# Twelve fp32r matmuls of four shapes in place of eight of the twelve bf16 warming matmuls, in an FNet mixing and feed-forward kernel

## The chip, the cores and the metric

One core of a Trainium2 chip. The time is the device time of one execution in microseconds, as a median over runs; the profile is of one execution, and its times count from the start of its span.

## What is computed

The input x is 2048 x 512, fp32. Two layers, each with a layer norm ahead and a residual around it:

```python
a = jnp.einsum("bsd,ed->bse", x, dft_hid_re)
b = jnp.einsum("bsd,ed->bse", x, dft_hid_im)
y = jnp.einsum("ts,bse->bte", dft_seq_re, a) - jnp.einsum("ts,bse->bte", dft_seq_im, b)
...
h = x + A(layernorm(x))                # A is the mixing above
h2 = h + (silu(layernorm(h) @ w1) @ w2)
```

The DFT matrices are inputs like any others: 2048 x 2048 for the sequence, 512 x 512 for the hidden dimension, each real and imaginary. w1 is 512 x 1792, w2 1792 x 512.

## The kernel before

The kernel keeps fp32 accuracy by splitting every operand into a rounded part and a remainder, both in fp32r, and forms each product by three matmuls: high weights with high moving data, high with low, low with high (`three`, lines 316 to 318). ScalarE makes the high part (line 266), VectorE the remainder (line 270, or 409 for the pieces of x). Every one of these matmuls has a weight tile of 128 x 128 and 512 moving columns. Block products are combined in the manner of Strassen: seven products in place of eight, with sums of blocks made on VectorE or by accumulating DMAs.

The stages follow each other on TensorE without a pause in the program: the mixing along the sequence (`plain(0, 0)`, then `fast` three times), the hidden mixing (`mix_fast`), and the up and down projections (`up`, `down`). A first part of `plain` takes the data as it arrives: the first tile of x and the first half-chunks of the sequence matrix are loaded (lines 468, 474 and 343), x is normalised (statistics at line 356, normalised high part at line 489, remainder at line 409), and TensorE does 4 + 4 + 4 products in three groups: high with high (line 513), high with the matrix's remainder (515), the remainder of x with high (517). Then it goes on with lines 316 to 318. `plain` then loads further pieces of x (line 343, `load_x`) and of the sequence matrix (line 442, `load_seq`), two of each per product.

The order of the work is written as events with times. `step` adds a stage of matmuls with work that leads it or follows it by so many microseconds; `at` adds a single piece of work. `MOVED` shifts each event by a number of its own, and the sorted list of events is the program's order, one and the same for all engines. Times in this list only sort; they make nobody wait.

Memory is 51 places of 4 KB per partition (`PAGES`). Every large tile is a "page". The program is run once against a stub, `Plan`, which notes for each page after how many uses it was requested and when it is used last by the list's times. `places` then gives each page, in the order of the requests, the free place that fell free earliest; fresh places come first:

```python
for taken, last in zip(self.taken, self.last):
    n = min((n for n in range(PAGES) if free[n][0] <= taken), key=lambda n: free[n][1])
    free[n] = last
```

A page in a used place waits at run time for the last reader of the page that was there before. A load that waits so holds up the SP queue, which issues nearly all loads, in order.

At the end of `program`, ahead of all events, come a few small pieces: three memsets on VectorE (`warm`, a bf16 tile of zeros, and two constants), one on GpSimd, and `WARM` = 12 matmuls of `warm` with itself into the first half of a PSUM tile `idle` that nobody reads (line 1357). They are the first work on TensorE.

Of the kernel before, what the change touches and what calls it, by code (L numbers as in the profile page):

```python
# [7 lines left out]
F32 = mybir.dt.float32  # L8
BF16 = mybir.dt.bfloat16
F32R = mybir.dt.float32r  # L10
# [5 lines left out]
P = 128  # L16
# [10 lines left out]
JJ = (2, 3, 0, 1)  # L27
EPS = 1e-5
PAGES = 51
WARM = 12  # L30
MM_US = 0.2265
PREP_US = 8.0
LEADS = (((0, 16, 8, 5.5), (1, 14, 5, 3.5), 12.5, 9),
# [149 lines left out]
class Plan:  # L183
# [5 lines left out]
    def page(self, name, dt=F32, shape=(2, 512)):  # L189
        self.taken.append(self.uses)  # L190
        self.last.append((self.uses, self.now))
        return Stub(self, len(self.taken) - 1)
# [14 lines left out]
def fnet_ffn_kernel(  # L207
# [18 lines left out]
    for plan.now, *_, f in program(stub, plan.page, stub, stub, stub, stub, x, xT, seq, hid, ffn, out):  # L226
        f()
    places = plan.places()

    def page(name, dt=F32, shape=(2, 512)):  # L230
        return pages.tile([P, *shape], dt, tag=f"pg{next(places)}", name=name)

    events = program(nc, page, keep, small, psum, dram, x, xT, seq, hid, ffn, out)


# [12 lines left out]
def program(nc, page, keep, small, psum, dram, x, xT, seq, hid, ffn, out):  # L248
# [11 lines left out]
    def banks(name):  # L260
        return psum.tile([P, 2, 512], F32, tag="ps", name=name)
# [1083 lines left out]
    up(1, 31, lambda: next(second[1]))  # L1345
    list(second[1])

    nc.vector.memset(warm, 0.0)
    nc.vector.memset(lower, -0.5 * EPS)
    nc.vector.memset(upper, EPS)  # L1350
    spare = keep.tile([P, 2], F32, name="spare")
# [3 lines left out]
    idle = banks("idle")  # L1355
    for _ in range(WARM):
        nc.tensor.matmul(idle[:, 0, :], warm[:, :P], warm, start=True, stop=True)

    return sorted(((t + MOVED.get(n, 0.0), at, n, f) for t, at, n, f in events), key=lambda v: v[:3])

# [33 lines left out]
```

## Time and profile before

| | us |
|---|---|
| median of 3 runs | 666.47 |
| lowest and highest run | 665.96, 666.97 |
| span of the profiled execution, first to last instruction | 664.2 |
| TensorE (PE) busy in that span | 657.6 |
| VectorE (DVE) busy | 575.7 |
| ScalarE (ACT) busy | 371.6 |
| GpSimd (POOL) busy | 97.8 |

The profile has one execution's instructions with start and length. "Busy" counts the time in which an engine executes, not that in which its sequencer waits or issues. PE is the matmuls, PEld the weight loads, which overlap them. A matmul's length in the profile is longer than its share of the engine, because the next one begins while it drains; the distance between two starts is what one costs. The span lies inside the device time; the profiled execution's own time outside the profiler isn't known, so the span of 664.2 us stands beside the median of 666.47 us, 2.3 us apart.

### The profile page before, as it was taken

What the parts mean: (1) busy time and instruction counts of PE and PEld (TensorE: products, weight loads), DVE (VectorE), ACT (ScalarE), POOL (GpSimd) and SP (SyncE); (2) the same over time, 40 slices, a digit from 0 to 9 for tenths busy, and PEclk for the clock granted to TensorE, in tenths of its full rate; (3) what the DMA queues carried; (4) which work ended last, traced back from release to release, by engine and by line L of the source; (5) the groups of instructions that cost most, each with busy time, mean ns of one, the idle gap of its engine ahead of it and who ended that gap; (6) DMA issues with size and microseconds to landing.
All of it is one profiled execution on the core that took longest, in us unless ns stands there. A gap on an engine that the chain in (4) does not pass through costs nothing.

```text
span 664.2 us, 8287 instructions
## 1 busy us (share of the span) xinstructions
PE 657.6 (99%) x2892; PEld 541.8 (82%) x2892; DVE 575.7 (87%) x727; ACT 371.6 (56%) x476; POOL 97.8 (15%) x128
## 2 busy tenths in 40 slices
PE   8999999999999999999999999999999999999997
PEld 5888888888888888888888888888888888888885
DVE  7999989898988999989999998988998854379964
ACT  6997456655445435364674555778543555664600
POOL 0011011111003434111121005343010000000000
PEclk9999999999999999999999999999999999999999
DMA  8981899999799586999999987669979645278803
GB/s 319 376 224 47 269 357 384 303 291 300 271 365 368 160 295 136 385 321 402 318 331 416 408 317 269 239 224 322 331 282 367 233 141 198 80 256 319 311 32 128
DMA packets 59706, 184.22 MB, mean 277 GB/s; under 512 B 6800, under 2 KB 13840, under 8 KB 59664
## 3 DMA queue, kind: packets, MB, share of 16 engines
q1 hardware_dynamic: 45456, 132.79, 54.8%
q0 software_dynamic: 13920, 50.63, 24.1%
q8 instruction: 23, 0.38, 0.3%
q10 hardware_dynamic: 288, 0.26, 0.1%
q14 instruction: 19, 0.16, 0.1%
HBM read 139.34 MB, written 44.32 MB: 277 GB/s over the span
## 4 chain that ended last, share of the span: by engine, by line
PE 98%; DMA 0%; DVE 0%; ACT 0%; issue 0%; DVEq 0%
PE m L317 11%; PE m L316 11%; PE m L318 11%; PE y L316 8%; PE y L318 8%; PE y L317 8%; PE f L318 6%; PE f L316 6%; PE f L317 6%; PE c L317 4%; PE c L318 4%; PE c L316 4%; PE vx L316 3%; PE vx L318 3%; PE vx L317 3%; PE c L517 1%
## 5 line engine op out<-in xcount | busy, mean ns | idle before, releaser
L266 ACT ACTIVATE ph<-raw 128x1024 fp32r<-128x1024 f32 x102 | 106.0, 1056 | 87.5 <-PE m L318 23.4
L270 DVE TENSOR_TENSOR pl<-raw,ph 128x1024 fp32r<-128x1024 f32 x88 | 112.1, 1289 | 9.1 <-ACT ph L266 7.1
L316 PE MATMUL m<-ph,S 128*128 128x512 f32 x192 | 74.7, 389 | 0.0
L317 PE MATMUL m<-pl,S 128*128 128x512 f32 x192 | 74.7, 389 | 0.0
L318 PE MATMUL m<-ph,S 128*128 128x512 f32 x192 | 74.7, 389 | 0.0
L316 PE MATMUL f<-gth,wf 128*128 128x512 f32 x161 | 62.6, 389 | 0.0
L317 PE MATMUL f<-gtl,wf 128*128 128x512 f32 x161 | 62.6, 389 | 0.0
L318 PE MATMUL f<-gth,wf 128*128 128x512 f32 x161 | 62.6, 389 | 0.0
L266 ACT ACTIVATE gth<-g 128x1024 fp32r<-128x1024 f32 x42 | 42.7, 1053 | 32.6 <-DVE g L1208 31.6
L270 DVE TENSOR_TENSOR gtl<-g,gth 128x1024 fp32r<-128x1024 f32 x42 | 50.3, 1219 | 7.0 <-ACT gth L266 5.7
L316 PE MATMUL m<-ph,X 128*128 128x512 f32 x144 | 56.0, 389 | 0.0
L317 PE MATMUL m<-pl,X 128*128 128x512 f32 x144 | 56.0, 389 | 0.0
L318 PE MATMUL m<-ph,X 128*128 128x512 f32 x144 | 56.0, 389 | 0.0
L1079 DVE TENSOR_TENSOR g<-vx,g 128x512 f32<-128x512 f32 x28 | 19.3, 689 | 30.5 <-PE vx L318 17.9
L714 DVE TENSOR_TENSOR raw<-raw,raw 128x1024 f32<-128x1024 f32 x36 | 43.9, 1221 | 0.5
L316 PE MATMUL y<-ph,hf 128*128 128x512 f32 x112 | 43.6, 389 | 0.0
L317 PE MATMUL y<-pl,hf 128*128 128x512 f32 x112 | 43.6, 389 | 0.0
L318 PE MATMUL y<-ph,hf 128*128 128x512 f32 x112 | 43.6, 389 | 0.0
L316 PEld LDWEIGHTS m<-ph,S 128*128 128x128 f32 x192 | 36.0, 188 | 7.5
L318 PEld LDWEIGHTS m<-ph,S 128*128 128x128 f32 x192 | 36.0, 188 | 7.5
L317 PEld LDWEIGHTS m<-pl,S 128*128 128x128 f32 x192 | 36.0, 188 | 7.4
L317 PEld LDWEIGHTS f<-gtl,wf 128*128 128x128 f32 x161 | 30.2, 188 | 6.3
(407 smaller groups left out, 1540.0 us busy)
## 6 DMA issues: line engine op xcount, KB each, us to landing
raw<-in_seq SPq DMA_DIRECT2D x84, 512.0 KB, 6.8
hf<-fd SPq DMA_DIRECT2D x28, 512.0 KB, 7.3
wf<-wd SPq DMA_DIRECT2D x28, 512.0 KB, 5.8
wf<-wd SPq DMA_DIRECT2D x28, 384.0 KB, 5.4
sf<-sd SPq DMA_DIRECT2D x18, 512.0 KB, 6.0
raw<-in_seq POOLq DMA_DIRECT2D x16, 512.0 KB, 6.9
fd<-hf POOLq DMA_DIRECT2D x14, 512.0 KB, 7.8
w<-in_ffn SPq DMA_DIRECT2D x23, 256.0 KB, 5.2
```

The costliest lines, as they stand in the source:

```text
L266: nc.scalar.activation(hi, src, AF.Copy, scale=sign)
L270: nc.vector.tensor_tensor(lo, src, hi, op=ALU.subtract)
L316: nc.tensor.matmul(acc, wh, mh, start=first, stop=False, skip_group_check=on)
L317: nc.tensor.matmul(acc, wh, ml, start=False, stop=False, skip_group_check=on)
L318: nc.tensor.matmul(acc, wl, mh, start=False, stop=last, skip_group_check=on)
L517: nc.tensor.matmul(o, wl, mh, start=False, stop=last)
L714: nc.vector.tensor_tensor(o, a, b, op=ALU.subtract)
L1079: nc.vector.tensor_tensor(g[q, f][:, tau, :], src, g[q, f][:, tau, :], op=ALU.add)
```

## The change

The twelve bf16 warming matmuls become four, unchanged in shape (128 x 128 weights, 512 columns). Behind them stand twelve new ones in fp32r, three of each of four shapes, written as (rows of weights, columns of weights, moving columns): (128, 128, 256), (128, 64, 512), (64, 128, 512), (128, 128, 512). They write the second half of the same PSUM tile, and nobody reads it. Their operand is the first half of a new page, `full`, which VectorE fills with zeros between the memset of `warm` and the two constants. The page comes from the same 51 places and is requested ahead of all others. The events and their order don't change.

```diff
-WARM = 12
+WARM = 4
+FORMS = (P, P, 256), (P, 64, 512), (64, P, 512), (P, P, 512)
...
+    full = page("full", F32)[:, 0, :]
     nc.vector.memset(warm, 0.0)
+    nc.vector.memset(full, 0.0)
+    full = full.bitcast(F32R)
     nc.vector.memset(lower, -0.5 * EPS)
     nc.vector.memset(upper, EPS)
...
     idle = banks("idle")
     for _ in range(WARM):
         nc.tensor.matmul(idle[:, 0, :], warm[:, :P], warm, start=True, stop=True)
+    for k, m, n in FORMS:
+        for _ in range(3):
+            nc.tensor.matmul(idle[:m, 1, :n], full[:k, :m], full[:k, :n], start=True, stop=True)
```

## The prediction

> **What bounds the kernel.** I read the page first: the span, the busy shares, the chain that ended last.
>
> ```profile
> span 664.2 us, 8287 instructions
> ...
> PE 657.6 (99%) x2892; PEld 541.8 (82%) x2892; DVE 575.7 (87%) x727; ACT 371.6 (56%) x476; POOL 97.8 (15%) x128
> ...
> PE 98%; DMA 0%; DVE 0%; ACT 0%; issue 0%; DVEq 0%
> ```
>
> TensorE is the bound, and 98% of the chain is matmuls. The next question is whether TensorE ever waits; the view of waits, for PE alone, answers it for the whole run:
>
> ```profile
> PE idle L1357 <- DVE upper L1350: 1.2, 1, 1.2
> PE c L513 <- DVE X L489: 0.5, 1, 0.5
> ```
>
> Two idle stretches: 1.2 us before the first warming matmul, 0.5 us between the warming and the first real one. So the case lies in the first ten microseconds, which the timeline shows (start, length, engine, line, operation, and in brackets the idle time before it and who ended it):
>
> ```profile
> 0.85 0.27 DVE L1348 MEMSET warm<- 128x256 uint32 x1 [0.85 <-PEq L1387]
> 1.18 4.23 PE L1357 MATMUL idle<-warm 128*128 128x512 bf16 x12 [1.18 <-DVE upper L1350]
> 1.58 0.15 PEld L1357 LDWEIGHTS <-warm 128*128 128x128 bf16 x1 [0.28 <-issue]
> 2.86 0.15 PEld L1357 LDWEIGHTS <-warm 128*128 128x128 bf16 x1 [0.28 <-issue]
> 3.26 0.75 DVE L356 BATCH_NORM_STATS2 st<-x 128x6 f32<-128x256 f32 x2 [2.12 <-DMA x<-in_x]
> 4.14 0.77 PEld L1357 LDWEIGHTS <-warm 128*128 128x128 bf16 x4 [0.28 <-issue]
> 5.35 0.73 DVE L489 TENSOR_SCALAR X<-x,mv,rs 128x256 fp32r<-128x256 f32 x2
> 5.91 1.17 PE L513 MATMUL c<-ph,X 128*128 128x512 f32 x4 [0.50 <-DVE X L489]
> 6.91 1.11 PE L515 MATMUL c<-pl,X 128*128 128x512 f32 x4
> 8.01 0.77 PEld L517 LDWEIGHTS c<-ph,X 128*128 128x128 f32 x4 [0.43 <-DVE X L409]
> 8.01 1.20 PE L517 MATMUL c<-ph,X 128*128 128x512 f32 x4
> 9.05 0.40 PE L316 MATMUL c<-ph,X 128*128 128x512 f32 x1
> ...
> 658.93 0.39 PE L318 MATMUL f4b<-gth,wf 128*128 128x512 f32 x1
> ```
>
> The weight loads start with their matmuls, so their starts give the pitch. While cold it is (4.14 - 1.58)/6 = 0.427 us; the four loads from 4.14 on lie in 0.77 us together, at most 0.77/3 = 0.26 us apart, about the half. So the rate doubled close to 4.15 us, 2.97 us after the first matmul. The column of the granted clock doesn't show this, so I trust the pitch:
>
> ```profile
> 2.00:4.00 2.00, 2.00 (x6) 0.76 (x5) 0.74 (x2) 0.64 (x2) 0.00 (x0) 1.00 0.78 266
> ```
>
> Of the 2880 real matmuls twelve start before 9.05 and the last at 658.93: 649.88/2867 = 0.2267 us each without a stall, to the end. Hence the rule of this case: **what moves the matmul at 9.05 moves the end by as much, and nothing before it counts.** From 5.91 to 9.05 are 3.14 us for 12 matmuls that need 12 x 0.2267 = 2.72; 0.42 us is slack. A first real matmul as late as 9.05 - 2.72 = **6.33 us** costs nothing. Nor can an earlier one gain: the third group starts at 8.01 because its weights, X, come from VectorE then, and VectorE's chain (statistics of x from 3.26 on, released by a DMA) doesn't contain TensorE.
>
> **The change part by part.** *The memsets.* 256 words took 0.27 us, so the new page's 512 take about 0.54 and VectorE is free at about 1.7 instead of 1.14 us. Its next work is at 3.26, behind a DMA: cost 0, cover 1.6 us. The first four matmuls need the old tile only, the fp32r ones the page, at 2.86 us: cover 1.2 us. If the first four waited for it as well, everything would begin 0.54 later.
>
> *The matmuls.* The four kept run cold from 1.18 to 2.86. The trace has no 256-column matmul and no cold fp32r weight load. Bounds: columns alone, half of 0.427, is 0.213 each; the price of a full one is 0.427. Warm, an fp32r load takes 188 ns:
>
> ```profile
> L316 PEld LDWEIGHTS m<-ph,S 128*128 128x128 f32 x192 | 36.0, 188 | 7.5
> ```
>
> Cold it is an estimate between 188 and twice that; I take 0.28 us each, load-bound, and 3.70 us for the end of the three (3.50 to 4.14 by the bounds). The other nine have 512 columns each; a half-filled array streams as many columns, so I price them as full ones, 0.427 cold and 0.2267 warm (halving the rows or columns of weights gives no reason for a gain, since the load lies under the stream). With the clock up at 4.15: 0.45/0.427 = 1.05 of them are through by then, 7.95 x 0.2267 = 1.80, the end at **5.95 us**; by the bounds 5.85 and 6.19. Before, the twelve ended at 1.18 + 4.23 = 5.41. So the idle half microsecond at 5.4 to 5.9 is filled, the first real matmul starts at about 5.95, its group waits for X at 8.01 again, and the matmul at 9.05 stays. All three values lie under 6.33: **0 us**, with 0.14 to 0.48 us of cover left.
>
> The page "TensorE: Matmul & The Clock Gate" of the Trainium skill, section "LDWEIGHTS (loading the stationary operand)", puts a load at its columns over 1.2 GHz, 107 ns for 128, an estimate under which the three would be bound by their columns and the warming end at 5.85 us. The trace's 188 ns disagrees, and the measurement decides; the kernel's end is the same by both.
>
> *The page.* The planner hands each new page the place freed earliest. The new one is first and holds a place, so the first 50 others take fresh places as before, the 51st, which had the last fresh one, now takes a used one, and the eleven after it a place freed one page later; then the page of a hid load takes the zeros' place and the old order is back, up to swaps between pages freed within one matmul of another, 0.23 us. Of the twelve, two are loads, which SP issues the moment the place is free. The rows for these and the hid load (SP's issues and waits, then DVE and ACT):
>
> ```profile
> 24.79 0.38 SPq L343 DMA_DIRECT2D x<-in_x  x1
> 32.03 0.33 SPq L442 DMA_DIRECT2D raw<-in_seq  x1
> 37.94 0.33 SPq L781 DMA_DIRECT2D hid<-in_hid  x1
> ```
> ```profile
> SPq L442 <- DVE pl L270: 6.7, 1, 6.7
> SPq L781 <- ACT xc L385: 5.5, 1, 5.5
> SPq L343 <- ACT xc L385: 3.4, 1, 3.4
> ```
> ```profile
> 29.65 2.35 DVE L270 TENSOR_TENSOR pl<-raw,ph 128x1024 fp32r<-128x1024 f32 x2
> ...
> 36.92 1.28 DVE L356 BATCH_NORM_STATS2 st<-x 128x6 f32<-128x512 f32 x2
> ```
> ```profile
> 30.02 1.51 ACT L385 ACTIVATE xc<-x,rs 128x512 f32<-128x512 f32 x2
> ...
> 36.41 1.51 ACT L385 ACTIVATE xc<-x,rs 128x512 f32<-128x512 f32 x2
> ...
> 43.36 1.99 ACT L266 ACTIVATE ph<-raw 128x1024 fp32r<-128x1024 f32 x2
> 46.05 1.52 ACT L385 ACTIVATE xc<-x,rs 128x512 f32<-128x512 f32 x2 [0.70 <-issue]
> ```
>
> Ten are first written by an engine, and late after the new predecessor's release; the closest is xc at 36.41, whose new predecessor is read last by ACT until 30.02 + 1.51 = 31.53, 4.9 us earlier. The load of x (tile group 3, second half) at 24.79 will wait for the first of the two DVE operations from 29.65, which ends at 30.87; the raw load at 32.03 will wait for ACT until 36.41 + 1.51 = 37.92; the hid load, in the zeros' place, follows at once. On SP nothing else stands between 24.79 and 37.94. So one load moves by 6.1 us and one by 5.9. Their times to landing, asked of the three issues one by one:
>
> ```profile
> DMA to landing us min/median/max: 9.5/9.5/9.5
> ```
> ```profile
> DMA to landing us min/median/max: 4.2/4.2/4.2
> ```
> ```profile
> DMA to landing us min/median/max: 5.6/5.6/5.6
> ```
>
> The first stood behind a full queue (34.3 landed); I price the moved ones by the other two. x: 30.89 + 4.2 to 5.6 = 35.1 to 36.5, read by DVE at 36.92: in time. Raw: 37.94 + 4.2 to 5.6 = 42.1 to 43.5, read by ACT at 43.36: at most 0.2 late, and ACT idles 0.70 before 46.05. **0 us.** The swaps move releases by 0.23 us in both directions; no input of TensorE after 30 us is written closer ahead of its use than this one, ready at 180.33, used at 180.64:
>
> ```profile
> 179.11 1.22 DVE L270 TENSOR_TENSOR pl<-c,ph 128x1024 fp32r<-128x1024 f32 x1
> ...
> 180.64 0.39 PE L317 MATMUL y<-pl,hf 128*128 128x512 f32 x1
> ```
>
> Its 0.31 us exceeds a swap's 0.23: 0.
>
> **Sum:** 0 + 0 + 0 on a span of 664.2. The median of 666.47 lies 2.3 us over that span (the runs from 665.96 to 666.97), and nothing of the change touches what lies around the span; I forecast **666.5 us**.
>
> **Rivals.** *The clock rises later (slower).* The rate doubled after 2.97 us of unbroken full-size matmuls. Now six of the twelve fill half the array and three are bound by their loads. If such matmuls don't count as work, counting begins with the last three: they start, cold, at 2.86 + 0.84 + 6 x 0.427 = 6.26, the warming ends at 7.54, 1.21 past the cover, and the clock rises at 6.26 + 2.97 = 9.23, so the real work runs 1.69 us at half rate and loses 0.85: +2.06, **668.5 us**. A rise just before 7.54 gives +1.2, 667.7; from a rise after 7.8 us the loss passes 1.33 us. For it: nothing in the trace shows that half-filled matmuls count. Against it: TensorE stays busy without a gap, and today's zeros suffice too. The page "TensorE: Matmul & The Clock Gate", Part 1, of the Trainium skill says that the gate watches a free-running window of 3.4 us and that the point varies from run to run. By that rule, as an estimate, the rise may fall up to 3.4 us later in some runs, and the longer warming, unlike today's, is then still going: up to about +1.2. The trace's one rise neither bears it out nor excludes it.
>
> *The moved loads are late (slower).* If the x load again takes 9.5 us it lands at 40.4, DVE is 3.5 late, and the next tight product reads S, written by DVE at 52.95 + 0.68, at 55.30:
>
> ```profile
> 52.95 0.68 DVE L409 TENSOR_TENSOR S<-s,S 128x512 fp32r<-128x512 f32 x1
> ...
> 55.30 0.39 PE L316 MATMUL c<-ph,S 128*128 128x512 f32 x1
> ```
>
> 1.67 us of cover, so up to +1.8: **668.3**. It decides from a landing after 38.6 us. Against: SP issues nothing from 24.79 on, so at 30.9 less is queued ahead.
>
> *TensorE changes its pace (faster).* Should fp32r or half-size matmuls at the start leave it in a state in which fp32r runs at half the cold pitch, 0.213, that is 2880 x 0.0132 = 38 us: **628**. For it: only the gap between 0.213 and 0.2267. Against: thousands of real fp32r matmuls keep exactly 0.2267 to the end; twelve more of the kind are nothing new.
>
> **How the numbers follow.** A measurement of this kernel can tell about 0.2%, 1.33 us. Forecast 0.75 (0.73 within 0.2%, 0.02 faster by scatter). Clock later 0.15: 0.05 with a rise under 7.8 us, within 0.2%; 0.10 beyond, slower. Late loads 0.05: 0.03 slower, 0.02 within. Pace 0.05, faster. Faster 0.07, same 0.80, slower 0.13. Range: the forecast's own 665.8 to 667.2 and the late rise up to 667.9; left out are the restarted clock (0.10), the pace (0.05) and the ends of the others (0.03).
>
> **What would show it.** Right: weight loads 0.427 us apart up to a rise near 4.15, the last fp32r warming matmul ending near 6.2 with no idle time before L513, the first L316 at 9.05, the SP loads at about 30.9 and 37.9, PE waits after 9.05 none. Wrong: a first L316 later than 9.1, a pitch other than 0.2267, a PE wait at 36 to 60 us, or a rise after 4.5.

## The result and the profile after

| | before | after |
|---|---|---|
| median of 7 runs each on the same chip, us | 666.32 | 669.00 |
| lowest and highest | 665.96, 667.10 | 667.05, 669.72 |
| ratio on record, with its 95% interval | | 1.0029 (1.002 to 1.0038) |
| profiled execution: its time, its span | span 664.2 | 667.1, span 665.3 |

The ratio here and below is the one on record. It lies close to the ratio of the means, 668.30/666.45 = 1.0028; the two medians alone would give 669.00/666.32 = 1.0040.

The change costs time. The forecast of 666.5, no change, was wrong, and 669.0 lies outside its range. The seven runs are two groups: 667.05, 667.05, 667.10, and then 669.00, 669.04, 669.16, 669.72. With the further runs of the same kernel below (12 timed and three single ones) 15 of 22 lie between 666.75 and 667.78 and seven between 668.95 and 670.05, with nothing in between; the middle of all 22 is 667.35. So there are two things to explain: a lower group some 0.7 us above the kernel before, and an upper group 2 us above that. The profiled execution belongs to the lower group.

The page of the changed kernel, its span, busy times and chain:

```profile
span 665.3 us, 8306 instructions
...
PE 658.7 (99%) x2896; PEld 543.1 (82%) x2896; DVE 575.8 (87%) x728; ACT 371.7 (56%) x476; POOL 97.8 (15%) x128
...
PE 98%; DMA 1%; DVE 0%; SPq 0%; issue 0%; ACT 0%
```

TensorE is the bound as before, and 1.1 us are added to the span. The waits of PE in the changed kernel:

```profile
PE idle L1361 <- DVE warm L1350: 1.2, 1, 1.2
```

The half microsecond ahead of the first real matmul is gone, filled by warming, as predicted. The start in the timeline of the changed kernel (start, length, engine, line, operation; the line numbers of the work are one higher than before, and in the kernels below with a larger kept tile two higher):

```profile
1.18 0.48 DVE L1351 MEMSET full<- 128x512 f32 x1
1.18 1.89 PE L1361 MATMUL idle<-warm 128*128 128x512 bf16 x4 [1.18 <-DVE warm L1350]
2.43 1.30 PEld L1364 LDWEIGHTS idle<-full 128*128 128x128 f32 x5 [0.28 <-issue]
3.93 0.22 PEld L1364 LDWEIGHTS idle<-full 128*64 128x64 f32 x1 [0.20 <-issue]
4.61 0.52 PEld L1364 LDWEIGHTS idle<-full 64*128 64x128 f32 x3 [0.45 <-issue]
5.49 0.53 PEld L1364 LDWEIGHTS idle<-full 128*128 128x128 f32 x3 [0.36 <-issue]
6.29 1.09 PE L514 MATMUL c<-ph,X 128*128 128x512 f32 x4
7.12 0.69 DVE L357 BATCH_NORM_STATS2 st<-x 128x6 f32<-128x512 f32 x1 [0.28 <-DMA x<-in_x]
7.22 1.08 PE L516 MATMUL c<-pl,X 128*128 128x512 f32 x4
8.39 1.19 PE L518 MATMUL c<-ph,X 128*128 128x512 f32 x4
9.43 0.40 PE L317 MATMUL c<-ph,X 128*128 128x512 f32 x1
...
659.54 0.39 PE L319 MATMUL f4b<-gth,wf 128*128 128x512 f32 x1
...
660.84 0.36 ACTq L1267 DMA_DIRECT2D out<-r  x1
```

The first real matmul starts at 6.29 (5.91 before), the dense stretch at 9.43 (9.05), the last matmul at 659.54 (658.93), and from there to the end of the span are 665.3 - 659.54 = 5.8 us, where they were 664.2 - 658.93 = 5.3. So the added 1.1 us of this execution is 0.38 at the start, 659.54 - 658.93 - 0.38 = 0.23 on the way, and some 0.5 behind the last matmul. The first of them is no late warming: the third group (L518) waits for X, and X hangs on a load of x that released DVE at 7.12; before, DVE came to this step at 6.73 without waiting. The loads that the prediction spoke of, from SP's rows of the changed kernel:

```profile
31.15 0.38 SPq L344 DMA_DIRECT2D x<-in_x  x1
38.16 0.33 SPq L443 DMA_DIRECT2D raw<-in_seq  x1
38.59 0.56 SPq L782 DMA_DIRECT2D hid<-in_hid  x1
```

They moved as forecast (30.9, 37.95, at once), and PE has no stall near them. Of the 0.23 us on the way 0.19 lie at 284 us, in the timeline of the changed kernel:

```profile
283.19 1.22 DVE L271 TENSOR_TENSOR pl<-raw,ph 128x1024 fp32r<-128x1024 f32 x1
284.16 0.39 PE L317 MATMUL m<-ph,X 128*128 128x512 f32 x1
284.46 0.19 PEld L318 LDWEIGHTS m<-pl,X 128*128 128x128 f32 x1 [0.34 <-DVE pl L271]
284.46 0.50 PE L318 MATMUL m<-pl,X 128*128 128x512 f32 x1
284.80 0.40 PE L319 MATMUL m<-ph,X 128*128 128x512 f32 x1
```

The matmuls' starts are 0.30 and 0.34 apart instead of 0.227: the remainder `pl` is ready only at 284.41, and the load of it as weights waits 0.34 us for that.

### The profile page after: what moved, and what is told of

It reads as the page before. It is cut to its first block, busy times and chain, and to the rows that moved or that the text cites. A ratio compares the mean times of both kernels' runs of the same rounds, so it can differ in the third digit from the quotient of the medians.

```text
span 665.3 us, 8306 instructions
## 1 busy us (share of the span) xinstructions
PE 658.7 (99%) x2896; PEld 543.1 (82%) x2896; DVE 575.8 (87%) x728; ACT 371.7 (56%) x476; POOL 97.8 (15%) x128
## 4 chain that ended last, share of the span: by engine, by line
PE 98%; DMA 1%; DVE 0%; SPq 0%; issue 0%; ACT 0%
PE m L319 11%; PE m L318 11%; PE m L317 11%; PE y L319 8%; PE y L317 8%; PE y L318 8%; PE f L318 6%; PE f L319 6%; PE f L317 6%; PE c L317 4%; PE c L319 4%; PE c L318 4%; PE vx L319 3%; PE vx L318 3%; PE vx L317 3%; DMA x<-in_x 1%
## 5 line engine op out<-in xcount | busy, mean ns | idle before, releaser
L317 PEld LDWEIGHTS f<-gth,wf 128*128 128x128 f32 x161 | 30.2, 188 | 6.3
```

What stands on the lines that cost most here:

```text
L317: nc.tensor.matmul(acc, wh, mh, start=first, stop=False, skip_group_check=on)
```

## The experiments

The theory after this result: the upper group loses its time at the start, because TensorE's rate doubles later in some runs, and some of the new matmuls don't count towards it. The rivals: the page of zeros, which shifts every later page's place; and the fp32r warming being longer. "Doubled at" below is where the trace's record of the granted rate begins; the distances between weight loads agree with it to one load. "Ratio" is against the kernel before, timed again with each series, which had medians of 666.30 to 666.51.

**The changed kernel again**, nothing edited.

> The changed kernel once more, as it is. Its seven runs fell into two groups, 667.05 to 667.1 and 669.0 to 669.72 us. Theory 1, the clock: in the upper group TensorE's rate doubles later than 4.2 us, so that the cold warming matmuls and the first real ones take longer; a profile of such a run shows weight loads 0.427 us apart beyond 4.5 us and the first L317 matmul some 2 us later than the 9.43 us of the profiled run, with no waits of TensorE afterwards beyond 0.2 us. Theory 2, the places: the start is as in the profiled run, and the 2 us are waits of TensorE after 30 us, behind loads that wait for a page. Both expect two groups again, about 667 and 669.

667.43 median of 12, ratio 1.0019 (1.0009 to 1.0029); nine runs from 666.95 to 667.78, three from 668.95 to 670.05. Two groups, in a second series on another occasion: they are the kernel's own.

**The zeros in a kept tile**, no page, the same sixteen matmuls:

```diff
-    warm = keep.tile([P, 512], BF16, name="warm")
+    full = keep.tile([P, 512], F32, name="warm")
+    warm = full[:, :256].bitcast(BF16)
...
-    full = page("full", F32)[:, 0, :]
...
-    nc.vector.memset(full, 0.0)
-    full = full.bitcast(F32R)
+    nc.vector.memset(full[:, 256:], 0.0)
+    r = full.bitcast(F32R)
...
-            nc.tensor.matmul(idle[:m, 1, :n], full[:k, :m], full[:k, :n], start=True, stop=True)
+            nc.tensor.matmul(idle[:m, 1, :n], r[:k, :m], r[:k, :n], start=True, stop=True)
```

> The sixteen warming matmuls of the change, but the zeros lie in the small tile that is kept all the time, and no page is taken: the pages lie as in the kernel before. Theory 1, the clock: the two groups stay, 667 and 669, the median 668 to 669. Theory 2, the places: the kernel before, 666.0 to 667.1, in one group, and no wait of TensorE at 284 us.

667.11 of 11, ratio 1.0008 (1.0000 to 1.0017): ten runs from 666.41 to 667.23 and one at 668.98. The lower group came down; that the upper one is nearly gone spoke for the page, and was a matter of too few runs, as the last experiment shows.

**The page alone**: twelve bf16 matmuls as before, reading the new page.

```diff
-WARM = 4
-FORMS = (P, P, 256), (P, 64, 512), (64, P, 512), (P, P, 512)
+WARM = 12
...
-    full = full.bitcast(F32R)
+    full = full.bitcast(BF16)[:, :512]
...
-        nc.tensor.matmul(idle[:, 0, :], warm[:, :P], warm, start=True, stop=True)
-    for k, m, n in FORMS:
-        for _ in range(3):
-            nc.tensor.matmul(idle[:m, 1, :n], full[:k, :m], full[:k, :n], start=True, stop=True)
+        nc.tensor.matmul(idle[:, 0, :], full[:, :P], full, start=True, stop=True)
```

> The twelve bf16 warming matmuls of before, unchanged in shape and number, but reading a page of zeros that is requested first and used as often as in the change, so that all pages lie as in the changed kernel. Theory 1, the clock: the kernel before, 666.0 to 667.1. Theory 2, the places: two groups as in the changed kernel, 667 and 669.

667.29 of 11, ratio 1.0012 (1.0003 to 1.0020), none above 668.28. It was a poor control: the page is cleared second, so TensorE starts at 1.72 us instead of 1.18. But its profile is worth more than its time: all twelve matmuls ran cold and the rate doubled only at 7.37 us, though nothing in the twelve differs from before but their start and the tile that they read:

```profile
1.72 0.13 PEld L1360 LDWEIGHTS <-full 128*128 128x128 bf16 x2 [1.72 <-DVE upper L1353]
6.39 1.36 PEld L513 LDWEIGHTS c<-ph,X 128*128 128x128 f32 x4 [0.28 <-issue]
```

The rate can rise only at the end of a window of 3.413 us (worked out at the end of this section). The window before ended at 3.96. By then the array had been busy for 3.96 - 1.72 = 2.24 us, and that did not suffice. In the profile of the changed kernel's second series the rate doubled at 3.82, after 3.82 - 1.18 = 2.64 us of work (three 256-column matmuls and 0.3 us of a 64-column one among it). So the point is no fixed time after the first matmul; the prediction's 2.97 us was one draw.

**All twelve at full size**, fp32r, in the kept tile.

```diff
-FORMS = (P, P, 256), (P, 64, 512), (64, P, 512), (P, P, 512)
+FORMS = ((P, P, 512),) * 4
```

> Zeros in the kept tile, pages as before, four bf16 matmuls and then twelve fp32r ones that all have 128 x 128 weights and 512 columns: no half-filled array, none bound by its load. Theory 1 in its form that partial matmuls don't count as work: the rate doubles at 4.2 us in every run, one group, and a first L317 at 9.1 to 9.4 us: 666.0 to 667.3. Theory 1 in its form that the rate doubles at a point that varies from run to run and the longer warming is in the way: two groups or a spread, up to 669. Theory 2, the places: 666.0 to 667.1.

667.09 of 11, ratio 1.0008 (0.9999 to 1.0017), none above 667.66. Longer warming without half-filled arrays, and no upper group, though the rate doubled at 5.39 in its profile and the first real matmul started at 6.81.

**One shape at a time**, twelve of it, kept tile: 64 columns of weights (the diff); 64 rows of weights, `((64, P, 512),) * 4`; 256 moving columns, `((P, P, 256),) * 4`.

```diff
-FORMS = (P, P, 256), (P, 64, 512), (64, P, 512), (P, P, 512)
+FORMS = ((P, 64, 512),) * 4
```

> Zeros in the kept tile, pages as before; four bf16 matmuls and twelve fp32r ones that all use 64 of the 128 columns of the array, 512 moving columns. Theory A: the rate doubles at the end of a window of 3.41 us in which the array was used enough, and a half-filled array counts less; then no window is full enough before the real matmuls, every run is late: the profile shows weight loads 0.427 us apart to the end of the warming near 8 us and a doubling at 9 us or later, and the runs take 668.5 to 671 us. Theory B: only occupancy counts, and the doubling comes at 3.6 to 7.0 us wherever a window ends: 666.4 to 667.7 us in all runs, as with twelve full ones.

> The same with 64 of the 128 rows of the array in place of the columns. Theory A, if rows count as columns do: 668.5 to 671 us in all runs, doubling at 9 us or later. Theory A with columns alone: 666.4 to 667.7. Theory B: 666.4 to 667.7 in all runs.

> The same with twelve full-array fp32r matmuls of 256 columns in place of the half-filled ones. In the profiles so far the second and third of such came 0.213 us apart while cold. Theories A and B both: the array is full, the doubling comes at 3.6 to 7.0 us, the warming ends by 5.8 us: 666.0 to 667.2. If short matmuls too count less, the doubling is late in some runs and these take 668 us or more.

| twelve of | median, us | ratio | runs | doubled at, us |
|---|---|---|---|---|
| 128 rows, 64 columns | 666.90 | 1.0007 (0.9998 to 1.0016) | 666.37 to 667.47 | 7.21 |
| **64 rows**, 128 columns | **670.00** | **1.0053 (1.0041 to 1.0066)** | 669.61 to 670.44 | **11.67** |
| 128 rows, 128 columns, 256 moving | 666.60 | 1.0001 (0.9992 to 1.0010) | 666.11 to 667.10 | 5.53 |

This is the experiment that decides. The timeline of the kernel with twelve 64-row matmuls:

```profile
3.00 4.77 PEld L1364 LDWEIGHTS idle<-warm 64*128 64x128 f32 x12 [0.84 <-issue]
3.00 5.49 PE L1364 MATMUL idle<-warm 64*128 64x512 f32 x12
8.41 1.35 PEld L515 LDWEIGHTS c<-ph,X 128*128 128x128 f32 x4 [0.65 <-ACT rs L290]
9.86 1.61 PEld L517 LDWEIGHTS c<-pl,X 128*128 128x128 f32 x4
11.57 0.94 PEld L519 LDWEIGHTS c<-ph,X 128*128 128x128 f32 x4
12.77 0.40 PE L318 MATMUL c<-ph,X 128*128 128x512 f32 x1
```

TensorE is occupied without a pause from 1.18 us, yet the groups of four real loads still take 1.35 and 1.61 us, the cold length, and fall to 0.94 only at 11.57. The kernel with 64 columns in place of 64 rows, whose rate came late in that run too:

```profile
6.71 0.22 PEld L1364 LDWEIGHTS idle<-warm 128*64 128x64 f32 x1 [0.20 <-issue]
7.13 0.17 PEld L1364 LDWEIGHTS idle<-warm 128*64 128x64 f32 x1 [0.20 <-issue]
7.41 0.89 PEld L515 LDWEIGHTS c<-ph,X 128*128 128x128 f32 x4
10.40 0.39 PE L318 MATMUL c<-ph,X 128*128 128x512 f32 x1
```

Loads are 0.42 apart up to 7.13 and then the real group takes 0.89: nothing but 64-column matmuls ran in the window that ended at 7.21, and they raised the rate. So half the rows don't raise it in a whole window, and half the columns do; matmuls of 256 columns do too (5.53). Whether these count in full, no run tells: in the run with 64 columns the window before ended at 7.206 - 3.413 = 3.79, with 3.79 - 1.18 = 2.61 us of work, 0.93 of it on 64 columns, and did not suffice, where 2.64 us did above.

**The page with an unchanged start**: the diff is against the kernel before; only the half of the page that the matmuls read is cleared, first of all.

```diff
+    full = page("full", F32)[:, 0, :]
+    full = full.bitcast(BF16)[:, :512]
+    nc.vector.memset(full, 0.0)
...
-        nc.tensor.matmul(idle[:, 0, :], warm[:, :P], warm, start=True, stop=True)
+        nc.tensor.matmul(idle[:, 0, :], full[:, :P], full, start=True, stop=True)
```

> The pages as in the changed kernel, twelve bf16 matmuls as before, and the memset of half a page put first, so that TensorE starts at 1.2 us as before (in the earlier trial of the page alone it started at 1.72). Theory 2, the places cost time of their own: the fastest runs lie at least 0.3 us over 665.9, a wait of TensorE stands in the profile after 30 us. Theory 1, the start is all: the kernel before, 665.9 to 667.2.

666.91 of 11, ratio 1.0008 (0.9999 to 1.0017), none above 667.50. The page alone makes no upper group; the run's fastest, 666.33, and its median lie 0.4 to 0.5 above the kernel before.

**The changed kernel without 64 rows, and with six of them**, page as in the change; the first line added is the one kernel, the second the other.

```diff
-FORMS = (P, P, 256), (P, 64, 512), (64, P, 512), (P, P, 512)
+FORMS = (P, P, 256), (P, 64, 512), (P, P, 512), (P, P, 512)
+FORMS = (P, P, 256), (64, P, 512), (64, P, 512), (P, P, 512)
```

> The changed kernel with its page and its places; only its three matmuls on 64 rows are full ones instead. Theory 1, half-filled rows don't count as use of the array and cost a window of 3.41 us where a window ends between 5.8 and 7.0 us: without them no run lies in the upper group, all of 666.9 to 667.9 us, median 667.1 to 667.4. Theory 2, the upper group comes of the places or of the longer warming: about 7 runs in 19 lie at 668.9 to 670.1 as before.

> The changed kernel with its page; the three matmuls on 64 columns are ones on 64 rows too, so that six in a row, from 3.5 to 6.1 us, don't fill the rows. Theory 1: a window now is full enough only if it ends by about 4.5 us, which leaves a quarter of the runs at 667 to 667.6 and puts three quarters at 668.5 to 670.3, median about 669.3. Theory 2: as the changed kernel, about 7 in 19 at 668.9 or more, median 667.5.

Without: 667.20, ratio 1.0015 (1.0006 to 1.0024), ten runs from 666.91 to 667.75 and one at 668.84. With six: 669.54, ratio 1.0041 (1.0026 to 1.0055), 666.64 and five runs from 668.92 to 670.18. The upper group follows the number of 64-row matmuls: 1 of 11, 7 of 22, 5 of 6. The one run at 668.84 is not explained.

**96 rows**, twelve of them, kept tile.

```diff
-FORMS = (P, P, 256), (P, 64, 512), (64, P, 512), (P, P, 512)
+FORMS = ((96, P, 512),) * 4
```

> Zeros in the kept tile, pages as before, four bf16 matmuls and twelve fp32r ones on 96 of the 128 rows. If the monitor counts rows in proportion and a window needs about 0.7 of full use, 96 rows just pass: as twelve full ones, 666.5 to 667.7, or a mixture. If only a full array counts: 669.6 to 670.4 in all runs, as on 64 rows.

666.86 of 11, ratio 1.0010 (1.0002 to 1.0019), none above 667.91. Doubled at 7.40, at the end of a window in which only 96-row matmuls ran, so these suffice; the real loads then run at full rate from the first:

```profile
2.44 5.02 PEld L1364 LDWEIGHTS idle<-warm 96*128 96x128 f32 x12 [0.28 <-issue]
7.50 0.88 PEld L515 LDWEIGHTS c<-ph,X 128*128 128x128 f32 x4
```

**The kernel before with 64 rows**: its twelve bf16 matmuls on half the rows, nothing else.

```diff
-        nc.tensor.matmul(idle[:, 0, :], warm[:, :P], warm, start=True, stop=True)
+        nc.tensor.matmul(idle[:, 0, :], warm[:64, :P], warm[:64], start=True, stop=True)
```

> The kernel before, its pages and its twelve bf16 warming matmuls, but all on 64 of the 128 rows of the array; no fp32r. Theory 1: rows decide and not the type; the warming runs cold to its end at 6.3 us, the real matmuls start cold, and the rate doubles when they alone have filled a window, at 8.7 to 12.2 us: 667.2 to 669 us in all runs, weight loads 0.427 us apart all through the warming. If fp32r is needed for the effect: the kernel before, 665.9 to 667.2.

668.37 of 5, ratio 1.0031 (1.0019 to 1.0043), from 668.31 to 669.08. Its timeline:

```profile
5.42 0.14 PEld L1357 LDWEIGHTS <-warm 64*128 64x128 bf16 x1 [0.28 <-issue]
6.41 2.07 PE L513 MATMUL c<-ph,X 128*128 128x512 f32 x4
8.28 1.91 PE L515 MATMUL c<-pl,X 128*128 128x512 f32 x4
9.98 1.85 PE L517 MATMUL c<-ph,X 128*128 128x512 f32 x4
11.68 0.40 PE L316 MATMUL c<-ph,X 128*128 128x512 f32 x1
```

Every one of the three groups of real matmuls runs cold (2.07, 1.91, 1.85 us; before they took 1.17, 1.11, 1.20), and the dense stretch begins 2.63 us late. No page, no fp32r, no longer warming: halving the rows alone makes all five runs slower than any run of the kernel before in that series (at most 667.09).

**The upper group itself**: the changed kernel three times with a profile, and the kept tile with the sixteen matmuls timed again.

> The changed kernel once more, one profile. Theory (64-row matmuls don't count; the window's end falls anywhere): with a chance of 3/8 a run of 668.9 us or more, whose weight loads double their rate between 9.2 and 10.5 us and whose first L317 starts near 11; else a run of about 667.1, doubled by 5.8. Rival (the upper runs lose their two microseconds at the end or in a stall): a run of 668.9 or more with the doubling before 5.8 us.

> As the one before: a second look for a run of the upper group, with the same numbers: doubled at 9.2 to 10.5 us at 668.9 or more, doubled by 5.8 us at about 667.1.

> As the two before: a third look, with the same numbers: doubled at 9.2 to 10.5 us at 668.9 or more, doubled by 5.8 us at about 667.1.

> The same sixteen warming matmuls as in the changed kernel, zeros in a kept tile, timed again. Theory (what makes the upper group are the three 64-row matmuls, which stand here too): 3/8 of the runs at 668.5 us or more, about 4 of 11. Rival (the page of zeros is needed for it): 1 of 11 or fewer, as in its first series.

The three runs fell into the lower group: 667.21, 667.33, 666.75, doubled at 3.83, 4.12 and 4.77. The kept tile gave 666.98 of 11, ratio 1.0010 (1.0000 to 1.0019): eight runs from 666.17 to 667.48, three from 668.94 to 669.06, so 4 of 22 in all, and no page is needed for them. And its profile is of a run of 669.06. The timeline of this upper run, with the same sixteen matmuls as the changed kernel:

```profile
3.94 0.22 PEld L1364 LDWEIGHTS idle<-warm 128*64 128x64 f32 x1 [0.20 <-issue]
4.92 0.93 PEld L1364 LDWEIGHTS idle<-warm 64*128 64x128 f32 x3 [0.76 <-issue]
6.49 0.93 PEld L1364 LDWEIGHTS idle<-warm 128*128 128x128 f32 x3 [0.65 <-issue]
7.52 1.61 PEld L515 LDWEIGHTS c<-ph,X 128*128 128x128 f32 x4
7.94 1.91 PE L515 MATMUL c<-ph,X 128*128 128x512 f32 x4
9.22 1.27 PEld L517 LDWEIGHTS c<-pl,X 128*128 128x128 f32 x4
10.54 0.87 PEld L519 LDWEIGHTS c<-ph,X 128*128 128x128 f32 x4
11.67 0.39 PE L318 MATMUL c<-ph,X 128*128 128x512 f32 x1
```

The warming runs cold to its end, three loads in 0.93 us against 0.52 above; the real work begins cold at 7.94, and the rate doubles at 10.05. The dense stretch starts at 11.67, 2.09 later than the 9.58 of the same kernel's lower run, and the span is 667.3 against 665.2. That is the whole difference between the groups, seen in one run of the kept tile; no run of the upper group with the page has a profile.

The two rises also show what sets the point. At its end each run loses the rate again, in the view by stretches of the changed kernel's lower run:

```profile
662.00:664.00 2.00, 0.00 (x0) 0.00 (x0) 0.00 (x0) 0.00 (x0) 0.00 (x0) 0.74 0.24 78
```

and of the upper run of the kept tile:

```profile
664.00:666.00 2.00, 0.00 (x0) 0.00 (x0) 0.00 (x0) 0.00 (x0) 0.00 (x0) 0.85 0.39 130
```

The last three numbers are the granted clock, the DMA share and GB/s. A clock of 0.74 over two microseconds is full rate to 662.96 and half after it; 0.85 is full rate to 665.40. From the rises at 4.17 and 10.05 these are 658.8 and 655.4 us. By the trace's record of the granted rate the stretch at full rate lasts 658.772 us in fourteen of the eighteen profiles and 655.359 us in the other four, and nothing else occurs. The two differ by 3.413 us and are 193 and 192 times that: rise and fall lie on one grid of 3.413 us, which starts anywhere in a run.

## Why the prediction was wrong, point by point

**The step that failed** is in the matmuls: "a half-filled array streams as many columns, so I price them as full ones", together with "With the clock up at 4.15". Half-filled by columns that holds. Half-filled by rows it holds for the stream (0.427 us each, cold) but not for the clock: 64-row matmuls, fp32r or bf16, didn't let the rate rise. In the upper run this made the matmuls' term, summed as 0 us, one of 11.67 - 9.05 = 2.62 us. And 4.15 was one draw: among the profiles here the rise comes at 3.8 to 7.4 us where 64 rows don't interfere, at the first end of a window of 3.413 us in which the array did enough, and somewhere between 2.24 and 2.64 us of work begins to suffice. In the upper run above the three 64-row matmuls and their switches take the time from 4.92 to about 6.4. An estimate from that, with 64-row matmuls at nothing and all others in full: a window that ends at 5.8 to 7.0 us has at most 4.92 - (5.8 - 3.41) = 2.5 us of full work ahead of them or too little behind them; the window before it ended by 3.6, with at most 3.6 - 1.18 = 2.4 us; both are lost, and the next ends at 9.2 to 10.4. If the grid started evenly, that would be (7.0 - 5.8)/3.41, 35% of the runs; the sixteen matmuls gave 11 of 44, seven of 22 with the page and four of 22 without. The 18 rises seen don't lie evenly on the grid, so the share isn't settled. The run at 10.05, whose lost window ended at 6.63, lies where it should. That the middle one of the first seven runs lay in the upper group was chance in part, with 7 of 22 there in all; the step would have been as wrong with 667.1.

**The first rival** was this mechanism: +2.06 us priced, 2.09 measured between the groups in the one kernel of which both have a profile. That the two agree is luck in part: the rival counted from the 9.05 of the kernel before, and from there the upper run is 2.62 late: about 7.94 - 6.33 = 1.61 by its warming, priced at 1.21, and (10.05 - 7.94)/2 = 1.06 by the real work at half rate, priced at 0.85. It had the argument "nothing in the trace shows that half-filled matmuls count" on its side and got a chance of 0.10 beyond 0.2%; seven of 22 runs and most of the first seven took it. Its details were half right: the 64-column and the 256-column matmuls count, and nothing has to be counted afresh from the last three. The page "TensorE: Matmul & The Clock Gate" of the Trainium skill, Part 1, says that a free-running window of 3.4 us decides; the grid of 3.413 us bears that out. The same part gives in one place a scatter of 0.5 us from run to run for the point. The five profiles of the changed kernel alone, 3.82 to 4.77 us, lie within that, but its sixteen matmuls in the kept tile gave 4.21 and 10.05, and the measurement decides. The free-running window should have moved the chance more than the single rise of the trace of before, which could not show a scatter.

**The 256-column matmuls**: priced at 0.28, bounds 0.213 and 0.427. They run cold at 0.213 us, half of 0.427 for half the columns, and twelve of them make a warming that ends early and costs nothing (666.60).

**The end of the warming**, forecast at 5.95 and at most 6.19: the first real matmul came at 6.29 in the profile of the lower group. The term left out is the change of shape. In the profile shown, matmuls start 0.316 to 0.335 us apart on either side of each switch to and from 64 rows, and about 0.23 elsewhere at full rate, so a switch costs about 0.2 us. (From 64 to 128 columns they start 0.235 apart in the run with 64 columns, so it is the rows.) That kept to the cover of 6.33 in some runs (6.13, 6.23, 6.28, 6.29) and not in one (6.56, where the rate rose at 4.77).

**The start of the dense stretch**, forecast to stay at 9.05: 9.16 to 9.58 in five profiles of the changed kernel. In the profile shown it hangs on a load of x, not on the warming, and such a start is seen without the page and without 64 rows too (9.11 with the page and twelve bf16 matmuls, 8.88 with 256 columns, 9.55 with full ones). In the run whose first real matmul came at 6.56 it hangs on the warming: the twelve follow each other without a gap up to 9.31, 2.75 us later. That nothing counts but where this matmul stands held; that it stands at 9.05 did not, since it moves with that load and, past the cover, with the warming.

**The memsets** cost nothing, as forecast: 0.48 us, under the estimate of 0.54.

**The page**, forecast at 0: the loads that move were named rightly and cost nothing. "Its 0.31 us exceeds a swap's 0.23" took one profile's closest place for enough; at 284 us 0.19 were lost in the profile shown. But no page is needed for that. The same matmul waits in three of the nine profiles without the page as well, here in the kernel before with half the rows, and there 0.40 us are lost:

```profile
286.95 0.19 PEld L317 LDWEIGHTS m<-pl,X 128*128 128x128 f32 x1 [0.55 <-DVE pl L270]
```

A wait of TensorE between 36 and 60 us, which the prediction named as a sign of being wrong, stands at 53 us in three of the five profiles of the changed kernel, and 0.1 to 0.3 us are lost there. It is a wait for ScalarE, which reads the products c out of PSUM:

```profile
52.96 0.19 PEld L317 LDWEIGHTS c<-ph,X 128*128 128x128 f32 x1 [0.46 <-ACT C L566]
```

The kept tile has that wait without a page (at 53.24, 0.24 us lost), so no moved load is needed for it. All such stalls together, the time from the start of the dense stretch to the last matmul less 2867 times 0.22667 us, are 0.04 to 0.75 us in the five profiles of the changed kernel, and 0.3 to 0.5 in four of the nine kernels without the page, so they vary from run to run.

What remains is the end of the run, which the prediction didn't look at. From the last matmul to the end of the span are 5.60 to 5.79 us in all nine profiles with the page, 5.41 to 5.46 in all seven with the larger kept tile, 5.22 and 5.25 in the two with neither. The upper run of the kept tile has 5.42, so this has nothing to do with the groups. The last store is issued 1.30 us after the last matmul in all eighteen (660.84 - 659.54 in the changed kernel). What differs with the page is the time until it has landed. The last two stores before, in the changed kernel and in the kept tile's first series:

```profile
DMA to landing us min/median/max: 2.7/2.8/2.9
```
```profile
DMA to landing us min/median/max: 3.2/3.3/3.3
```
```profile
DMA to landing us min/median/max: 2.6/2.8/2.9
```

The last one lands 3.01 to 3.20 us after its issue in the nine profiles with the page and 2.61 to 2.67 in the nine without. So the page costs 0.3 to 0.6 us there; through what, no run here tells. The 0.2 us of the kept tile are another thing: its stores land as before, but the span ends 1.50 us after the last landing instead of 1.28 or 1.29, with VectorE's closing instruction 1.28 us after it instead of 0.81. Why is open too.

So the lower group's 0.7 us are some 0.5 behind the last matmul and the rest an average of a later start and short stalls; one of the three single runs, at 666.75, shows them apart, with no stall: dense from 9.31, last matmul at 659.21, 5.7 behind it. Why the start moved in the mean is not settled. No version tried is faster than the kernel before.

## What to carry to other kernels

Warm TensorE with matmuls on all 128 rows; they may be narrow or short, but half the rows left it cold here through more than 5 us without a pause (3.00 to 8.41). A change to the first ten microseconds has to be timed over many runs and its groups looked at one by one, for the rate may rise anywhere over several microseconds, and the one profile shows one draw. A chance for a rival should rest on what the trace excludes; a single event in one execution excludes little.

## What was not expected of the hardware

- The rows of a matmul count for the clock: 64 of 128 did not raise the rate in a whole window (rise at 11.67 and 11.64 us), 96 did (7.40). 64 of 128 columns on all rows did (7.21).
- Ninety-six rows count for less than 128, by this estimate: in the run with the rise at 7.40 the window before ended at 3.99 with 1.7 us of full work (1.18 to 2.86) and 1.1 of 96-row work and did not suffice, though 2.64 us of other work did in another run; so a 96-row microsecond is worth at most (2.64 - 1.7)/1.1 = 0.85 of a full one.
- A switch between 128 and 64 rows of weights costs about 0.2 us at full rate, two matmuls starting 0.32 and 0.335 us after the one ahead instead of 0.23.
- The same last store lands 3.0 to 3.2 us after its issue in all nine profiles of kernels with the page of zeros, and 2.6 to 2.7 in all nine without, though it is issued the same 1.30 us after the last matmul. The cause is open.
